# A decode kernel: the order of its first weight loads, and a first load of 14 KB rows

## The chip, the cores and the metric

The kernel runs on one core of one Trainium2 chip. The metric is the device time of one launch in microseconds (us). Times are quoted as medians, with the lowest and highest run. The profiled execution's span is about 1.2 us shorter than the time measured for the same run (399.1 us against 400.33), because the span goes from the first to the last instruction only.

## The reference, cut to what matters

One token goes through attention against a KV cache of 65536 positions (32 query heads, 4 KV heads), and through a mixer and MLP branch. Both results are added to the token.

```python
x  = layernorm(A_x)                                 # 1 x 1 x 1024
q  = x @ wq                                         # wq 1024 x 4096,   8.4 MB
o  = softmax(q k^T / sqrt(128)) v ; o @ wo          # k, v 67 MB each, wo 8.4 MB
h  = gelu(layernorm(x) @ w1)                        # w1 1024 x 1024,   2.1 MB
hs = shift(h) @ w2                                  # w2 1024 x 1024,   2.1 MB
x1 = x + hs
h2 = gelu(layernorm(x1) @ w3) @ w4                  # w3, w4            7.3 MB each
out = A_x + attention + x1 + h2                     # layer norms and details cut
```

The shift moves h along the sequence, by one or two places, and fills with zeros. The sequence has one position, so what reaches w2 is all zeros. The kernel still loads w2 and multiplies a vector of zeros with it. The values that lie in w2's place don't change the result as long as they are finite.

## The kernel before: the parts that matter

All large loads are issued by SyncE on one queue, so they run one after another on the core's 16 DMA engines. x (2 KB) is issued by ScalarE on a second queue. `KV` has three slots of 64 KB per partition; the weights go into them first, and each slot is given to K or V as soon as its weights have been used.

```python
def rows_src(w, r0, nrow):        # partition p gets rows 8p .. 8p+7, one contiguous run of memory
    return w.rearrange("(p r) n -> p (r n)", p=P)[:, r0 * w.shape[1]:(r0 + nrow) * w.shape[1]]

_dma(q_act, chan("x"), ... out=x_bf, in_=A_x ...)                        # 16 B per partition
kv_load(0, "s0", rows_src(A_wq, 0, 8), 8 * HQD)                          # wq: 64 KB per partition
kv_load(1, "w1", rows_src(B_w1, 0, 8), 8 * D, b_w1)                      # w1: 16 KB
_dma(q_sp, chan("w2"), ... out=KV[:, 1, 8*D:16*D], in_=rows_src(B_w2, 0, 8) ...)   # w2: 16 KB
kv_load(2, "s2", rows_src(B_w3, 0, 8), 8 * F)                            # w3: 56 KB
# ... (cut) layer norm of x, q = xn @ wq, then:
issue(3)                          # first K block into slot 0, after wq was used
# ... (cut) w1, gelu, w2 (with zeros)
issue(4)                          # first V block into slot 1
# ... (cut) w3, gelu
issue(5)                          # second K block into slot 2
# ... (cut) 8 blocks of attention; each issues the loads two blocks ahead
# ... (cut) at the end wo and four parts of w4: 17, 7, 3 and 1 row per partition
```

## Time and profile before

| | before |
|---|---|
| time, median (lowest to highest) | 400.36 us (400.35 to 400.61) |
| span | 399.1 us |
| moved by DMA | 169.97 MB, 426 GB/s over the span |
| DMA busy | 9 tenths or more in nearly every slice |
| DVE / PE busy | 55% / 42% |

The first lines of the page, with the row of 40 slices for DMA. Each digit is the busy share of a slice of 10 us in tenths. PE is TensorE's matmuls and PEld its weight loads, DVE is VectorE, ACT is ScalarE, POOL is GpSimd; SPq and ACTq are the queues of instructions that issue loads.

```profile
span 399.1 us, 3429 instructions
...
PE 168.9 (42%) x1523; PEld 59.0 (15%) x1484; DVE 221.4 (55%) x260; ACT 23.9 (6%) x50; POOL 7.7 (2%) x31
...
DMA  9999899999999999999999999999999999999995
GB/s 420 420 388 493 383 441 466 447 415 427 420 427 429 434 460 434 434 427 420 434 427 420 466 440 434 421 420 434 427 427 466 434 440 420 420 427 434 418 414 229
DMA packets 3759, 169.97 MB, mean 426 GB/s; under 512 B 548, under 2 KB 552, under 8 KB 808
```

DMA never rests and no other engine comes near. In the trace's packet records one packet is one partition's row of a load, so 64 KB for wq, K and V. A 64 KB packet takes a median of 2.42 us, and 16 engines at that rate move 434 GB/s. This agrees with the ceiling of 435 GB/s that the Trainium skill gives in "DMA: Bandwidth & Descriptors", Where 436 GB/s comes from.

The timeline of the early part of the kernel before. The columns are start in us, duration in us, engine, line, operation, output and input; in brackets the idle time of the engine before it and what ended it.

```profile
0.00 0.39 SPq L290 DMA_DIRECT2D KV<-in_A_wq_dram  x1
0.12 0.37 ACTq L295 DMA_DIRECT2D KV<-in_A_x_dram  x1
0.92 0.33 SPq L290 DMA_DIRECT2D KV<-in_B_w_dram  x1
1.30 0.73 SPq L300 DMA_DIRECT2D KV<-in_B_w_dram  x1
2.08 0.48 SPq L290 DMA_DIRECT2D KV<-in_B_w_dram  x1
...
22.24 0.17 DVE L339 CAST KV<-KV 128x8 f32<-128x8 bf16 x1 [22.24 <-DMA KV<-in_A_x_dram]
...
27.53 4.98 PE L379 MATMUL S_ps<-KV 128*32 128x512 bf16 x64 [1.36 <-DVE KV L359]
...
69.47 0.33 SPq L290 DMA_DIRECT2D KV<-in_A_k_cache_dram  x1
...
99.84 0.33 SPq L290 DMA_DIRECT2D KV<-in_A_v_cache_dram  x1
100.21 0.43 SPq L290 DMA_DIRECT2D KV<-in_A_k_cache_dram  x1
```

Although x has only 2 KB, it lands after 22.1 us, with wq. The q projection (27.53) waits for the layer norm of x. The lines at 69.47 and 100.21 show the slack of this early chain: the loads issued at 99.84 and 100.21 are wanted only as the engines finish the second K block, the first of them at 105.8 and the last at 107.7 us; it counts as landed at 108.2.

The chain of waits of the kernel before, in order of time: start in us, duration in us, what it was.

```profile
0.12 22.10 DMA KV<-in_A_x_dram
69.47 38.72 DMA KV<-in_A_k_cache_dram
108.21 13.10 DVE KV L460 x3
138.97 46.66 DMA KV<-in_A_k_cache_dram
185.65 13.10 DVE KV L460 x3
...
263.26 13.10 DVE KV L460 x3
...
363.64 32.91 DMA KV<-in_B_w_dram
```

Each block of attention starts when its K has landed, and the last thing waited for is w4. Its last row:

```profile
396.60 0.28 PE L566 MATMUL S_ps<-KV,gh_bf 128*1 128x256 bf16 x4 [0.15 <-DMA KV<-in_B_w_dram]
396.94 0.42 DVE L647 CAST orow<-S_ps 128x256 bf16<-128x256 f32 x1 [6.78 <-PE S_ps L566]
```

### The profile page before, as it was taken

The numbers are of one execution on the slowest core, as the hardware profiler recorded it, in microseconds if no ns is written. First come the engines' busy times: TensorE is split into PE (matmuls) and PEld (weight loads), VectorE is DVE, ScalarE is ACT, GpSimd is POOL, SyncE is SP. The second block draws the span as 40 slices with busy tenths as digits, with TensorE's granted clock in tenths as the row PEclk, the third lists the DMA queues.
The fourth block names the chain that finished last, engine by engine and source line by source line (L and its number), as shares of the span: only waits on it lengthen the run. The fifth ranks groups of instructions, "written<-read, shape, count | busy, mean of one in ns | idle before, by whom it ended". The sixth has DMA issues, their size and how long they took to land.

```text
span 399.1 us, 3429 instructions
## 1 busy us (share of the span) xinstructions
PE 168.9 (42%) x1523; PEld 59.0 (15%) x1484; DVE 221.4 (55%) x260; ACT 23.9 (6%) x50; POOL 7.7 (2%) x31
## 2 busy tenths in 40 slices
PE   0034767338033713460357036413541362137394
PEld 0011334012001210110012001101120110012232
DVE  0024222994298549833984597269647952895201
ACT  1000000011001100110011002000100110011000
POOL 5000000000000000000000000000000000000000
PEclk9998568555655665575557555855585558555969
DMA  9999899999999999999999999999999999999995
GB/s 420 420 388 493 383 441 466 447 415 427 420 427 429 434 460 434 434 427 420 434 427 420 466 440 434 421 420 434 427 427 466 434 440 420 420 427 434 418 414 229
DMA packets 3759, 169.97 MB, mean 426 GB/s; under 512 B 548, under 2 KB 552, under 8 KB 808
## 3 DMA queue, kind: packets, MB, share of 16 engines
q1 hardware_dynamic: 3608, 169.87, 98.7%
q8 instruction: 5, 0.08, 0.1%
q10 hardware_dynamic: 144, 0.00, 0.0%
q14 instruction: 2, 0.02, 0.0%
HBM read 169.87 MB, written 0.00 MB: 426 GB/s over the span
## 4 chain that ended last, share of the span: by engine, by line
DMA 59%; DVE 25%; PE 12%; issue 1%; ACT 1%; SPq 1%; POOL 0%
DMA KV<-in_A_k_cache_dram 45%; DVE KV L460 18%; DMA KV<-in_B_w_dram 8%; DMA KV<-in_A_x_dram 6%; PE S_ps L411 3%; PE OT_ps L518 2%; DVE mrow L481 2%; PE M_ps L426 2%; PE S_ps L474 2%; PE S_ps L379 1%; ACT p_sb L496 1%; DVE Yall L395 1%; DVE pT_f L509 1%; DVE pT_f L419 1%; PE PT_ps L505 0%
## 5 line engine op out<-in xcount | busy, mean ns | idle before, releaser
L460 DVE STREAM_TRANSPOSE KV<-KV 128x4096 f32<-128x4096 f32 x32 | 140.3, 4422 | 44.3 <-DMA KV<-in_A_k_cache_dram 44.3
L474 PE MATMUL S_ps<-KV,Ycur 128*32 128x512 bf16 x512 | 60.7, 624 | 132.5 <-DVE KV L460 132.5
L518 PE MATMUL OT_ps<-KV,pT_f 128*32 128x512 bf16 x512 | 47.2, 511 | 4.0 <-issue 3.0
L474 PEld LDWEIGHTS S_ps<-KV,Ycur 128*32 128x32 bf16 x512 | 14.3, 126 | 160.0 <-DVE KV L460 142.4
L496 ACT ACTIVATE p_sb<-S_ps,brun 128x1024 bf16<-128x1024 f32 x16 | 17.8, 1114 | 276.6 <-DVE brun L494 176.1
L509 DVE STREAM_TRANSPOSE pT_f<-PT_ps 128x512 f32<-128x512 f32 x32 | 22.5, 702 | 14.0 <-PE PT_ps L505 14.0
L481 DVE TENSOR_REDUCE mrow<-S_ps 128x1 f32<-128x1024 f32 x16 | 19.3, 1205 | 11.3 <-PE S_ps L474 11.3
L484 PE MATMUL M_ps<-Rm,Lmat 128*128 128x16 bf16 x16 | 3.1, 194 | 38.0 <-DVE Rm L482 38.0
L529 DVE SCALAR_TENSOR_TENSOR O_acc<-O_acc,ff,OT_ps 128x512 f32<-128x512 f32 x12 | 9.0, 748 | 14.7 <-PE OT_ps L518 14.7
L518 PEld LDWEIGHTS OT_ps<-KV,pT_f 128*32 128x32 bf16 x512 | 13.1, 115 | 23.8 <-issue 16.4
L411 PE MATMUL S_ps<-KV 128*32 128x512 bf16 x88 | 12.1, 538 | 2.7 <-DVE KV L359 2.7
L339 DVE CAST KV<-KV 128x8 f32<-128x8 bf16 x1 | 0.2, 172 | 22.2 <-DMA KV<-in_A_x_dram 22.2
L578 PE MATMUL S_ps<-KV,o_bf 128*1 128x512 bf16 x64 | 9.9, 484 | 4.5 <-DMA KV<-in_A_wo_dram 4.5
L505 PE MATMUL PT_ps<-p_sb,permR 128*128 128x512 bf16 x16 | 9.7, 607 | 0.8
L426 PE MATMUL M_ps<-ident_f,pT_f 64*128 64x2 f32 (+2 forms) x32 | 7.9, 373 | 2.5 <-DVE pT_f L419 2.5
L484 PEld LDWEIGHTS M_ps<-Rm,Lmat 128*128 128x128 bf16 x16 | 1.7, 104 | 49.3 <-DVE Rm L482 49.3
L582 DVE COPY pT_f<-S_ps 1x512 f32<-1x512 f32 x1 | 0.7, 679 | 14.4 <-PE S_ps L578 14.4
L426 PEld LDWEIGHTS M_ps<-ident_f,pT_f 64*128 64x128 f32 (+2 forms) x32 | 7.7, 326 | 4.7 <-DVE pT_f L419 3.1
L419 DVE COPY pT_f<-S_ps 64x512 f32<-64x512 f32 (+1 forms) x3 | 2.1, 685 | 10.8 <-PE S_ps L411 10.8
L505 PEld LDWEIGHTS PT_ps<-p_sb,permR 128*128 128x128 bf16 x32 | 3.3, 102 | 27.5 <-ACT p_sb L496 14.7
L364 PE MATMUL M_ps<-KV 8*128 8x8 bf16 x1 | 0.2, 184 | 16.1 <-DVE Dmat_f L363 16.1
L642 POOL MEMSET pT_f<- 64x512 f32 x1 | 0.5, 520 | 312.4 <-PE OT_ps L518 312.4
(88 smaller groups left out, 90.2 us busy)
## 6 DMA issues: line engine op xcount, KB each, us to landing
KV<-in_B_w_dram SPq DMA_DIRECT2D x1, 7168.0 KB, 48.0
KV<-in_B_w_dram SPq DMA_DIRECT2D x1, 4352.0 KB, 27.4
KV<-in_B_w_dram SPq DMA_DIRECT2D x2, 2048.0 KB, 28.3
KV<-in_B_w_dram SPq DMA_DIRECT2D x1, 1792.0 KB, 31.3
KV<-in_B_w_dram SPq DMA_DIRECT2D x1, 768.0 KB, 32.7
KV<-in_B_w_dram SPq DMA_DIRECT2D x1, 256.0 KB, 32.9
KV<-in_A_k_cache_dram SPq DMA_DIRECT2D x8, 46.7
KV<-in_A_v_cache_dram SPq DMA_DIRECT2D x8, 28.1
```

Source lines behind the costliest of these rows:

```text
L411: fns.append(lambda e, j=j, k=k, mv=mv: e.matmul(S_ps[32 * (k % 4):32 * (k % 4) + 32, bank + k // 4, :], vec[:, j:j + 1].broadcast_to([P, ...
L419: _op(q_dve, lambda e, b=b, nb=nb: e.tensor_copy(pT_f[0:32 * nb, b, :], S_ps[0:32 * nb, bank + b, :]), reads=[b_S[bank + b]], writes=[b_pT ...
L426: fns.append(lambda e, b=b, nb=nb, c=c: e.matmul(M_ps[:, c0 + 16 * b + c:c0 + 16 * b + 4 * nb:4], pT_f[0:32 * nb, b, c:512:4], ident_f[0:3 ...
L460: _op(q_dve, lambda e: e.transpose(out=KV32[:, s, o:o + 4096], in_=KV32[:, s, o:o + 4096]), reads=[b_KV[s][sub]], writes=[b_KV[s][sub]], l ...
L474: fns.append(lambda e, we=we, cm=cm, mv=mv: e.matmul(S_ps[32 * cm:32 * cm + 32, n % 4, :], Ycur[:, we, :, :].rearrange("p a g -> p (a g)") ...
L481: _op(q_dve, lambda e: e.reduce_max(mrow[:, k:k + 1], S_ps[:, 2 * k:2 * k + 2, :].rearrange("p b c -> p (b c)"), axis=AX.X), reads=b_S[2 * ...
L496: _op(q_act, lambda e: e.activation(p_sb[:, :, :].rearrange("p b c -> p (b c)"), S_ps[:, 2 * k:2 * k + 2, :].rearrange("p b c -> p (b c)") ...
L505: _op(q_pe, lambda e: e.matmul(PT_ps[:, :], permR[:, :], p_sb[:, n % 2, :], start=True, stop=True), reads=[b_p[n % 2], b_const], writes=[b ...
L509: _op(q_dve, lambda e: e.transpose(out=pT_f[:, n % 2, :], in_=PT_ps[:, :]), reads=[b_PT], writes=[b_pT[n % 2]], loop=True)
L518: fns.append(lambda e, q=q, q4=q4: e.matmul(OT_ps[32 * q4:32 * q4 + 32, g % 2, :], pT_bf[:, n % 2, q, :, 1], KV[:, s, 8192 * sub + 512 * q ...
L529: _op(q_dve, lambda e: e.scalar_tensor_tensor(out=O_acc[:, 0:512], in0=O_acc[:, 0:512], scalar=ff[:, k:k + 1], in1=OT_ps[:, k, :], op0=ALU ...
L578: _grp(q_pe, [lambda e, j=j, jj=jj: e.matmul(S_ps[32 * jj:32 * jj + 1, 1, :], o_bf[:, j:j + 1], KV[:, 0, j * D + 512 * jj:j * D + 512 * (j ...
```

## The change

Its intent is a better start of the DMA stream. The first load is now seven of w2's eight rows per partition, 14 KB, so that neighbouring partitions read at an odd multiple of 2 KB and not at a power of two (this distance between the starts of neighbouring partitions' pieces is called stride or pitch below); then come wq, w1, w2's last row and w3. Since w2 only meets zeros, it need not matter that this division puts other rows into the partitions.

```diff
-        kv_load(0, "s0", rows_src(A_wq, 0, 8), 8 * HQD)
         b_w1 = b_KV[1][0:2]
         b_w2 = b_KV[1][2:4]
+        _dma(q_sp, chan("w2"), lambda e: e.dma_start(out=KV[:, 1, 8 * D:15 * D], in_=B_w2[0:7 * P, :].rearrange("(p r) n -> p (r n)", p=P)), writes=b_w2)
+        kv_load(0, "s0", rows_src(A_wq, 0, 8), 8 * HQD)
         kv_load(1, "w1", rows_src(B_w1, 0, 8), 8 * D, b_w1)
-        _dma(q_sp, chan("w2"), lambda e: e.dma_start(out=KV[:, 1, 8 * D:16 * D], in_=rows_src(B_w2, 0, 8)), writes=b_w2)
+        _dma(q_sp, chan("w2"), lambda e: e.dma_start(out=KV[:, 1, 15 * D:16 * D], in_=B_w2[7 * P:8 * P, :]), writes=b_w2, partial=True)
         kv_load(2, "s2", rows_src(B_w3, 0, 8), 8 * F)
```

## The prediction

> **What bounds the kernel now.** DMA. The page's slice row shows DMA at 9 nearly throughout; 169.97 MB over a 399.1 us span is 426 GB/s. In the trace's packet records the first load packet starts 1.02 us into the span, and from there to about 393 us the 16 engines are never short of packets. A 64 KB packet takes a median 2.421 us, so 16 engines move 434 GB/s and the bytes alone need 392 us. The chain of waits is 45% DMA of K and ends on w4's last row, landing at 396.6.
>
> **What the change moves.** The same bytes in another order: w2a (1.84 MB), wq, w1, w2's last row (0.26 MB), w3.
>
> 1. x lands earlier. Its 16 B packets, eight per engine, are on another queue. The Trainium skill, "DMA: Bandwidth & Descriptors", Queues, rings and completion order, says that an engine round-robins between queues packet by packet; the trace agrees: each x packet follows a 64 KB wq packet, and x lands at 22.1 us. Behind 14 KB packets (0.54 us each in w4's 7-row part) I estimate 6 to 7.
> 2. wq lands later by 8 x 0.54 = 4.3 us: 21.7 -> 25.9. The q projection starts there rather than at 27.53, so the early chain, to the gelu at 69.5, moves about 1.3 us earlier. That buys nothing: the next K and V loads are issued (100 us) 8 us before the DMA queue runs dry (K lands at 108.2), and all later work waits for DMA.
> 3. More packets: w2's eight 16 KB packets per engine (0.611 us) become eight of 0.539 and eight of 2 KB (0.084): 4.98 instead of 4.89 us, +0.1 us.
> 4. The start. The 16 first wq packets take 2.83 to 3.48 us instead of 2.42, 0.72 us too much on average, never regained. Some is first-read latency: 8 KB instruction fetches on the idle chip before the span took 0.34 to 0.55 us against 0.30 at full rate, so 0.04 to 0.25. The rest I lay to engines starting in step at addresses a power of two apart. The skill's same page (Latency and other measured facts, HBM row pitch) reports slow copies at pitches of 512 KiB and up; here a pitch of 64 KB runs at full rate once engines are staggered, so only the start can suffer. A 14 KB stride should remove about 0.5 us, unless it returns when wq starts.
>
> **Critical path.** Only 3 and 4 lie on it: -0.5 + 0.1 = -0.4 us. The tail stays: engines end their last loads between 394.0 and 396.1 us; the slowest carries its start lag (0.6 us) and 16 KB instruction fetches (1.0 to 1.1 us each).
>
> **Prediction: 399.9 us**, 8 in 10 within 399.2 to 400.7. Faster by over 2%: 0.01; within 2%: 0.98; slower by over 2%: 0.01.
>
> **What would show it.** x landing at 6 to 7 us; layer norm over by 13; q projection from about 26 us, begun by DMA instead of DVE; first 14 KB packets within 0.3 us of 0.54; the wq packets after them at 2.42; first K's transposes near 68.2; third K landing (108.2) 0.3 to 0.6 us earlier, and later ones by the same.
>
> **What would make it wrong.** If the slow start is plain latency, or reappears in wq's first packets: 400.4 to 400.5. If the slowest engine at the end was the one that lost most at the start, or instruction fetches fall on another engine, the gain may reach 1 us.

## The result, and the profile after

The changed kernel took 401.08 us (400.49 to 401.15, 4 runs) against 400.37 us (400.35 to 400.61, 4 runs). The ratio is 1.0013, with a 95% interval of 0.9996 to 1.0031. Ratios here are the mean time of one kernel's fast runs over that of the other's of the same rounds, so not quite the ratio of the medians. That is the same within 2%, but it lies on the other side of zero than predicted and above the range. Two repeats gave 401.09 us each, 0.72 and 0.57 us over the kernel before of the same rounds, so the loss of 0.6 to 0.7 us is real, if small.

The page after:

```profile
span 399.8 us, 3446 instructions
...
DMA  9999999999999999999999999999999999999995
GB/s 394 420 397 479 411 420 465 439 421 439 426 426 428 420 459 433 426 439 439 426 420 439 446 433 426 434 433 426 426 452 439 426 439 420 433 426 433 421 412 213
DMA packets 3903, 169.97 MB, mean 425 GB/s; under 512 B 564, under 2 KB 568, under 8 KB 952
```

The same bytes moved, and DMA is as busy as ever. The first slice moved 394 GB/s instead of 420. The timeline after, with the lines that answer to those above:

```profile
0.00 0.39 SPq L298 DMA_DIRECT2D KV<-in_B_w_dram  x1
...
0.91 0.33 SPq L290 DMA_DIRECT2D KV<-in_A_wq_dram  x1
1.30 1.13 SPq L290 DMA_DIRECT2D KV<-in_B_w_dram  x1
7.68 0.33 SPq L301 DMA_DIRECT2D KV<-in_B_w_dram  x1
...
10.12 0.17 DVE L340 CAST KV<-KV 128x8 f32<-128x8 bf16 x1 [10.12 <-DMA KV<-in_A_x_dram]
...
27.16 6.25 PE L380 MATMUL S_ps<-KV 128*32 128x512 bf16 x64 [13.12 <-DMA KV<-in_A_wq_dram]
...
70.79 0.33 SPq L290 DMA_DIRECT2D KV<-in_A_k_cache_dram  x1
...
100.35 0.33 SPq L290 DMA_DIRECT2D KV<-in_A_v_cache_dram  x1
100.72 0.43 SPq L290 DMA_DIRECT2D KV<-in_A_k_cache_dram  x1
```

x is now there at 10.12 instead of 22.24, and the q projection waits for wq and no longer for the layer norm. Yet it ends at 33.4 and not earlier than before (32.5), because its 64 matmuls took 6.25 us instead of 4.98; more on that below. The next K and V are issued at 100.35 and 100.72, still well before the queue needs them. So the early chain costs nothing, in either kernel. The chain of waits and the tail after:

```profile
0.91 26.11 DMA KV<-in_A_wq_dram
70.79 37.58 DMA KV<-in_A_k_cache_dram
108.40 13.10 DVE KV L461 x3
138.63 47.19 DMA KV<-in_A_k_cache_dram
185.84 13.10 DVE KV L461 x3
...
263.72 13.10 DVE KV L461 x3
...
364.10 33.24 DMA KV<-in_B_w_dram
```

```profile
397.38 0.28 PE L567 MATMUL S_ps<-KV,gh_bf 128*1 128x256 bf16 x4 [0.15 <-DMA KV<-in_B_w_dram]
397.71 0.42 DVE L648 CAST orow<-S_ps 128x256 bf16<-128x256 f32 x1 [7.78 <-PE S_ps L567]
```

K lands 0.19 us later at 108 and 186, 0.46 later at 264, and w4's last row 0.78 later. A constant start loss would give a constant delay. The packet records explain why it grows.

**Each of the 16 DMA engines has its own clock of progress.** The engines get equal shares of every large load and never wait for each other, so an engine that falls behind stays behind. How far each engine's last packet of a load lies behind the first engine's, in us, sorted; read from the packet records, which name no engine: the engines are told apart by which packet starts where another ended.

```
                    first engine   lag of the 16 engines
before, first K      67.07   0 0 .01 .07 .11 .13 .17 .18 .19 .28 .35 .53 .62  .63 1.14 1.96
before, second K    105.78   0 .01 .01 .07 .11 .13 .17 .19 .28 .36 .53 .62 .63 1.14 1.73 1.96
before, wo          376.83   0 0 .07 .11 .13 .16 .18 .28 .35 .53 .62 .62 1.54 1.72 1.96 2.11
before, w4, 17 rows 387.16   0 0 .06 .10 .16 .18 .27 .35 .52 .61 .62 1.53 1.66 1.72 1.95 2.10
after,  first K      67.34   0 .03 .03 .09 .10 .17 .17 .30 .44 .50 .69 .96 1.08 1.20 1.33 1.88
after,  second K    106.08   0 0 .06 .09 .11 .16 .28 .41 .47 .66 .94 1.05 1.14 1.31 1.53 1.86
after,  wo          377.12   0 .06 .08 .11 .15 .27 .41 .47 .66 .94 1.05 1.13 1.52 1.55 1.85 2.27
after,  w4, 17 rows 387.45   0 .06 .08 .11 .15 .27 .41 .47 .66 .94 1.13 1.52 1.55 1.85 2.27 2.59
```

The lags below 1.3 us come from the start. The large ones come from instruction fetches, which the trace records as packets of kind "instruction" on queues 8 and 14, on the same 16 engines: five of 16 KB and two of 8 KB in this span. Each 16 KB fetch puts its engine back by about 1.55 us (for instance .18 to 1.73 in the kernel before, fetch at 81.8), each 8 KB fetch by 0.97 (1.14 to 2.11). A load counts as landed when the last engine is done, so the end waits for the engine with the largest sum of start lag and fetches.

This accounts for the result. w4's last packet ended at 396.09 before and 396.88 after, 0.79 us later. Of that, 0.29 is the fastest engine (376.83 to 377.12), and 0.48 is the lag of the last one (2.11 to 2.59). The last engine after the change is the one that had left the start 1.05 us late and then took the 16 KB fetch at 378.2: its 1.05 is gone from the next row of the table, and 2.59 is new. In the kernel before the fetch at 378.2 met an engine that was 0.13 late (it is at 1.66 after it). So the start grew worse in two ways, in its mean and in its spread, and the fetches turned the spread into time at the end.

### The profile page after: what moved, and what is told of

It is laid out like the page before. It is cut to its first block, busy times and chain, and to the rows that moved or that the text cites. A ratio compares the mean times of both kernels' runs of the same rounds, so it can differ in the third digit from the quotient of the medians.

```text
span 399.8 us, 3446 instructions
## 1 busy us (share of the span) xinstructions
PE 177.4 (44%) x1539; PEld 60.3 (15%) x1484; DVE 221.3 (55%) x260; ACT 23.9 (6%) x50; POOL 7.6 (2%) x31
## 4 chain that ended last, share of the span: by engine, by line
DMA 59%; DVE 25%; PE 12%; issue 1%; ACT 1%; SPq 1%; POOL 0%
DMA KV<-in_A_k_cache_dram 45%; DVE KV L461 17%; DMA KV<-in_B_w_dram 8%; DMA KV<-in_A_wq_dram 7%; PE S_ps L412 3%; PE OT_ps L519 2%; DVE mrow L482 2%; PE M_ps L427 2%; PE S_ps L475 2%; PE S_ps L380 2%; DVE pT_f L510 1%; ACT p_sb L497 1%; DVE Yall L396 1%; DVE O_acc L530 1%; DVE pT_f L420 1%
## 5 line engine op out<-in xcount | busy, mean ns | idle before, releaser
L506 PE MATMUL PT_ps<-p_sb,permR 128*128 128x512 bf16 x32 | 18.4, 574 | 0.8
L412 PE MATMUL S_ps<-KV 128*32 128x512 bf16 x88 | 12.5, 565 | 2.7 <-DVE KV L360 2.7
L380 PE MATMUL S_ps<-KV 128*32 128x512 bf16 x64 | 6.2, 575 | 13.1 <-DMA KV<-in_A_wq_dram 13.1
L579 PE MATMUL S_ps<-KV,o_bf 128*1 128x512 bf16 x64 | 8.8, 442 | 3.1 <-DMA KV<-in_A_wo_dram 3.1
```

What stands on the lines that cost most here:

```text
L380: fns.append(lambda e, j=j, b=b, jj=jj: e.matmul(S_ps[32 * jj:32 * jj + 32, b, :], xn_bf[:, j:j + 1].broadcast_to([P, 32]), KV[:, 0, j * H ...
L412: fns.append(lambda e, j=j, k=k, mv=mv: e.matmul(S_ps[32 * (k % 4):32 * (k % 4) + 32, bank + k // 4, :], vec[:, j:j + 1].broadcast_to([P, ...
L506: _op(q_pe, lambda e: e.matmul(PT_ps[:, :], permR[:, :], p_sb[:, n % 2, :], start=True, stop=True), reads=[b_p[n % 2], b_const], writes=[b ...
L579: _grp(q_pe, [lambda e, j=j, jj=jj: e.matmul(S_ps[32 * jj:32 * jj + 1, 1, :], o_bf[:, j:j + 1], KV[:, 0, j * D + 512 * jj:j * D + 512 * (j ...
```

## The experiments

Theory S: the small first packets spoil the start. Rivals: O, the odd stride does harm; P, the division into two loads does; X, x's packets do; and, later, C, the compact source of the first load, and D, a first load from another tensor than the next. The times are beside the kernel before of the same rounds and chip. "Mean K" is the mean over the 16 engines of the end of the first K load; it shows the start without the luck of the fetches at the end. It comes from one profiled launch of each run; the three of the changed kernel gave 67.90, 67.90 and 67.80.

| run | first load | time, us (range) | before, us | difference | mean K, us |
|---|---|---|---|---|---|
| before | wq, 64 KB at 64 KB pitch | | | | 67.47 |
| changed kernel | w2, 14 KB at 14 KB | 401.08 (400.49-401.15) | 400.37 | +0.71 | 67.90 |
| after_again | the same | 401.09 (400.91-401.31) | 400.37 | +0.72 | 67.90 |
| after_third | the same | 401.09 (400.63-401.21) | 400.52 | +0.57 | 67.80 |
| x_behind | the same, x on one queue | 401.11 (400.99-401.56) | 400.42 | +0.69 | 67.95 |
| w2_whole_first | w2, 16 KB at 16 KB | 400.69 (400.47-400.89) | 400.37 | +0.32 | 67.68 |
| split_not_first | wq, then the divided w2 | 400.51 (400.36-400.52) | 400.37 | +0.14 | 67.51 |
| wq_row_first | wq, 8 KB at 64 KB | 400.37 (400.31-400.46) | 400.42 | -0.05 | 67.41 |
| wq_compact | wq, 14 KB at 14 KB | 400.78 (400.51-400.88) | 400.56 | +0.22 | 67.67 |
| wq_spread | wq, 14 KB at 64 KB | 400.58 (400.51-400.80) | 400.56 | +0.02 | 67.63 |
| k_pitch14 | K, 14 KB at 14 KB | 401.13 (400.98-401.20) | 400.52 | +0.61 | 67.78 |
| k_pitch16 | K, 14 KB at 16 KB | 401.13 (401.04-401.21) | 400.52 | +0.61 | 68.22 |
| k_pitch32 | K, 14 KB at 32 KB | 400.57 (400.44-400.99) | 400.52 | +0.05 | 67.59 |
| k_spread | K, 14 KB at 64 KB | 400.49 (400.33-400.79) | 400.56 | -0.07 | 67.55 |
| small_first | w2, 2 KB at 2 KB | 400.72 (400.53-402.02) | 400.42 | +0.30 | 68.24 |
| small_from_wq | wq, 2 KB at 64 KB | 401.97 (400.87-402.52) | 400.56 | +1.41 | 67.80 |
| w3_first | w3, 56 KB at 56 KB | 407.84 (407.17-408.64) | 400.37 | +7.47 | 67.61 |
| no_w2 | wq, w2 not loaded | 395.45 (395.41-395.70) | 400.42 | -4.97 | |

Most differences are so small that the 95% interval of the ratio holds 1. For the pairs that carry the argument the ranges of the runs are apart: k_pitch14 and k_pitch16 (lowest 400.98) against k_spread (highest 400.79), and against the kernel before of their own rounds (highest 400.68).

### after_again and after_third: does it repeat?

The changed kernel, unaltered.

> The changed kernel once more, to see whether its time and its start repeat. Theory S (small first packets make a worse start: the 16 DMA engines leave the start more spread out, and the end waits for the most delayed engine): about 401.0 us; after the wq load the last engine is 0.9 to 1.2 us behind the first (0.61 in the kernel before). If the 0.7 us was chance of one load of the program: 400.4 and a spread near 0.6.

> The changed kernel as a control on this chip: 0.6 to 0.8 us over the kernel before, mean end of the first K load near 67.9 us.

It repeats: +0.72 and +0.57 us. In after_again the last three engines that no fetch had touched were 1.00, 1.01 and 1.07 us behind after wq (0.52, 0.61, 0.61 in the kernel before). One run in 4 and one in 5 came out at 400.5 and 400.6, so the start varies from launch to launch; those launches were not profiled.

### split_not_first: the division alone

```diff
+        kv_load(0, "s0", rows_src(A_wq, 0, 8), 8 * HQD)
         _dma(q_sp, chan("w2"), ... 7 rows of w2 ...)
-        kv_load(0, "s0", rows_src(A_wq, 0, 8), 8 * HQD)
```

> wq first as in the kernel before, then the divided w2: wq, seven rows of w2, w1, w2's last row, w3. Theory S: 400.4 to 400.6 us (0.1 us for the added packets), spread after wq 0.6 us. Rival P: about 401.0.

+0.14 us, as estimated for the added packets, though the two ranges overlap. The 401.0 us of rival P are far off, so it falls.

### w2_whole_first and w3_first: other strides, nothing divided

```diff
-        kv_load(0, ... wq) ; kv_load(1, ... w1) ; _dma(... w2) ; kv_load(2, ... w3)
+        _dma(... w2) ; kv_load(0, ... wq) ; kv_load(1, ... w1) ; kv_load(2, ... w3)     # w2_whole_first
+        kv_load(2, ... w3) ; kv_load(0, ... wq) ; kv_load(1, ... w1) ; _dma(... w2)     # w3_first
```

> All eight rows of w2 first, undivided (16 KB packets, a power-of-two stride), then wq, w1, w3. Theory S: as the changed kernel, 400.8 to 401.2 us, spread after wq 0.9 to 1.2 us. Rival O (the odd 14 KB stride itself does the harm): 400.3 to 400.5, spread near 0.6. Rival P (dividing w2 into two loads does the harm, by more packets): 400.3 to 400.5. The change's intent (the odd stride helps): over 401.2.

> w3 first (56 KB packets, stride 7 x 8 KB), then wq, w1, w2, nothing divided. Theory S: large first packets, so a start like that of the kernel before: 400.2 to 400.6 us, spread after the first load near 0.6 us. Rival O and the step of my prediction that failed (the start costs 0.5 us because of a power-of-two stride): if the stride mattered, the first packets would be over their full-rate time by 0.2 us or less rather than by 0.6.

w2_whole_first came out in between, at +0.32 us, and fitted neither theory. In w3_first the start answers the question: its 56 KB packets, at a stride that is no power of two, were too long by 0.66 us each on average over the 16 engines. The kernel before lost 0.72 with its stride of 64 KB. So the slow first packets are no matter of a power-of-two stride, and this was the very step on which my gain of 0.5 us rested.

The time of w3_first was a miss of mine, and a useful one. wq landed at 38 us, the early chain ran 12 us later, and the next loads were issued at 110.92 and 111.29, when the queue had run dry. The windows of w3_first, with DMA share and GB/s last:

```profile
85.00:105.00 20.00, 9.54 (x76) 2.51 (x80) 18.20 (x13) 1.21 (x2) 0.00 (x0) 0.50 0.97 420
105.00:112.00 7.00, 5.59 (x64) 1.43 (x54) 3.33 (x9) 1.30 (x3) 0.00 (x0) 0.81 0.30 103
112.00:125.00 13.00, 3.80 (x32) 0.89 (x32) 13.00 (x4) 0.00 (x0) 0.00 (x0) 0.60 1.00 425
```

The share of 0.30 in the second line is the hole: 5.65 us without a packet for the mean engine. The early chain's slack ends when the engines finish the second K load, so in the kernel before it was 6 to 8 us (issue at 99.84, engines done between 105.8 and 107.7).

The same trace holds one thing more. When the queue began again, at 111.9 us, the first 16 packets, 64 KB each of V, took 2.58 to 3.44 us, too long by 0.68 on average, though another block of V had been read before. So slow first packets are not peculiar to the start of the launch: here they came back when all engines began together after a pause. (Hole and second start make 6.3 of the 6.8 us by which this profiled launch was longer.)

### wq_row_first: small packets, other place

```diff
-        kv_load(0, "s0", rows_src(A_wq, 0, 8), 8 * HQD)
+        _dma(q_sp, chan("s0"),  ... out=KV[:, 0, 0:HQD],         in_=rows_src(A_wq, 0, 1) ...)
+        _dma(q_sp, chan("wqb"), ... out=KV[:, 0, HQD:8 * HQD],   in_=rows_src(A_wq, 1, 7) ...)
```

> wq is divided instead of w2: its first row of each partition (8 KB packets at a power-of-two pitch of 64 KB), then its other seven rows (56 KB packets), then w1, w2, w3. Theory S (small first packets spoil the start, whatever the stride): 400.7 to 401.3 us; fastest engine 0.1 to 0.4 us later than in the kernel before, most delayed engine 0.8 us or more behind it. Rival O (the harm came from the odd stride of the load, or from w2's place): 400.3 to 400.6 and a spread near 0.6.

No loss at all (-0.05 us), with first packets of 8 KB. After the first K load only two engines, both hit by fetches, were more than 0.44 us behind. Theory S, my own, fell here.

### x_behind: x's packets

```diff
-        _dma(q_act, chan("x"), ...)
         _dma(q_sp, chan("w2"), ... 7 rows of w2 ...)
+        _dma(q_sp, chan("x"), ...)
```

> The changed kernel with x on the same queue, behind the seven rows of w2, instead of on a second queue. Rival X (packets of x that interleave with the first small packets spoil the start): 400.4 to 400.7, spread near 0.6. Theory S: 400.9 to 401.2, spread 0.9 to 1.1.

+0.69 us, as the changed kernel. Rival X falls.

### wq_compact, wq_spread, k_spread: the same first load from other places

Only the source of the first load is altered. Its shape, packets and destination stay, and the result stays correct because the data meet zeros.

```diff
-  in_=B_w2[0:7 * P, :].rearrange("(p r) n -> p (r n)", p=P)
+  in_= 1.8 MB from the head of wq in one piece, 14 KB per partition         # wq_compact
+  in_= rows_src(A_wq, 0, 8)[:, 0:7 * D]                                     # wq_spread, 64 KB pitch
+  in_= the first K block, the first 14 KB of each partition's 64 KB         # k_spread
```

> The changed kernel, but its first load takes the same shape (14 KB packets, 14 KB stride, 1.8 MB in one piece) out of the head of wq instead of w2. The data are multiplied by zeros, so the result stays correct. Theory D (the first reads of a tensor are slow, and a short first load of another tensor makes wq pay again): mean end of the first K load over the 16 engines 67.4 to 67.6 us (67.47 in the kernel before, 67.90 in the changed one), time 400.4 to 400.7. Rival C (all engines reading one compact 1.8 MB piece at the start): 67.8 to 68.0, 400.9 to 401.2. Rival S (small packets first) is already against wq_row_first.

> The same, with the 14 KB pieces taken from wq at a pitch of 64 KB, so spread over 8 MB. Theories C and D both: mean end of the first K load 67.4 to 67.6, time 400.4 to 400.7. If it is as slow as the changed kernel (67.8 or more, 401), both fall, and it is the 14 KB packets, or the place they are written to.

> The same, with the 14 KB pieces taken at a pitch of 64 KB from the K cache, another tensor than the wq that follows. Theory C (compactness): 67.4 to 67.6, time 400.4 to 400.7. Theory D (another tensor first): 67.8 to 68.0, time 400.9 to 401.2.

Taken at a pitch of 64 KB, the 14 KB pieces cost nothing, whether from wq (+0.02) or from another tensor (-0.07). So theory D falls, and it is not the 14 KB packets either. The compact piece out of wq cost +0.22, less than that out of w2. Even this is not clear of noise: the range of wq_compact (400.51 to 400.88) covers that of wq_spread, and their mean K is nearly the same, 67.67 and 67.63. For wq alone, theory C is not shown.

### k_pitch14, k_pitch16, k_pitch32: the pitch alone

The 14 KB pieces all come from the K cache, and the pitch is the only difference between these runs.

```diff
+  in_=A_k_cache[0, 0, 0:BLK, :].rearrange("c d -> (c d)")[0:P * 7 * D].rearrange("(p c) -> p c", p=P)[:, 0:7 * D]
   # k_pitch16: 8 * D in place of the first 7 * D; k_pitch32: 16 * D
```

> The changed kernel with its 14 KB pieces taken from the K cache at a pitch of 14 KB (compact, odd stride); k_spread took them at 64 KB and was as fast as the kernel before. Theory C (a compact source is slow at the start): 0.2 to 0.8 us over before. If 0.6 to 0.8, compactness in a tensor other than wq explains the changed kernel whole; if 0.2 to 0.4, like wq_compact, then something of w2 itself adds to it. Rival (not the source's layout, but chance): within 0.1 of before.

> The same 14 KB pieces at a pitch of 16 KB, a power of two, over 2 MB of the K cache. Theory C: as k_pitch14 within 0.15 us. The change's intent, and my prediction's step: the odd pitch is better, so this one is slower than k_pitch14 by 0.3 us or more. Rival O (an odd pitch is worse): faster than k_pitch14 by 0.3 or more.

> The same 14 KB pieces at a pitch of 32 KB, over 4 MB. Theory C: between k_pitch14 and k_spread, so 0.0 to 0.4 us over before.

In the K cache the pitch decides it: +0.61 us at 14 KB, +0.61 at 16 KB, +0.05 at 32 KB, and -0.07 at 64 KB (k_spread). Odd or even makes no difference; how close together the 16 engines read does. Where the last w4 row was used up and the output was copied, in k_pitch14 first and then in k_spread:

```profile
397.73 0.42 DVE L648 CAST orow<-S_ps 128x256 bf16<-128x256 f32 x1 [7.69 <-PE S_ps L567]
```

```profile
396.99 0.42 DVE L648 CAST orow<-S_ps 128x256 bf16<-128x256 f32 x1 [7.41 <-PE S_ps L567]
```

The changed kernel had this copy at 397.71, the kernel before at 396.94. So a compact source is enough for a loss as large as the changed kernel's. The two compact runs lose it in different ways. In k_pitch14, as in the changed kernel, some engines leave the start late, up to 1.3 us behind the first (1.1 in the changed kernel). Part of this is that they begin late: the last engine's first packet started at 2.56 us in k_pitch14 and at 2.87 in the changed kernel, against 1.62 in k_spread and 1.88 in the kernel before. It need not be so: in after_third none began later than 1.65, but the packets of the first load were too long by 0.90 us per engine. In k_pitch16 all engines leave it together, and all late: the fastest ended the first K load at 67.88 us instead of 67.07, and no engine without a fetch was over 0.39 behind.

### small_first and small_from_wq: a very short first load

```diff
+        _dma(q_sp, chan("w2"), ... w2's last row, 2 KB per partition ...)       # small_first
         kv_load(0, "s0", rows_src(A_wq, 0, 8), 8 * HQD)
         kv_load(1, "w1", ...)
+        _dma(q_sp, chan("w2a"), ... the other seven rows ...)
   # small_from_wq: the 2 KB come from wq at a pitch of 64 KB
```

> Only w2's last row first (2 KB packets, 0.7 us at full rate), then wq, w1, w2's seven rows, w3. If the start costs its delay once, after the first read, in whatever packets come then: 400.5 us (0.1 more than before for the packets). If a small first load makes the start be paid a second time, in the first packets of wq: 400.8 to 401.3, and the first 64 KB packets are over 2.42 us by 0.3 or more.

> small_first with its 2 KB pieces taken from wq at a pitch of 64 KB instead of from w2 (result still correct). small_first had a mean end of the first K load of 68.24 and wq's first packets 0.76 us too long on average. Theory D: wq has been touched, so its first 64 KB packets run near 2.42 us, mean end 67.4 to 67.7, time 400.4 to 400.7. If wq's first packets still cost 0.5 us or more, D falls: then a short first load is paid by whatever comes next.

Both vary much from launch to launch (400.53 to 402.02, and 400.87 to 402.52). The profiles are of the slowest launch of small_first (402.02) and the fastest of small_from_wq (400.87). In them the first wq packets were too long by 0.74 and 0.48 us per engine, after the 2 KB packets had already lost 0.36 and 0.23. A first load of 0.7 us is over before the start is, and what follows pays again, even at a pitch of 64 KB. This is a second way to lose at the start; theory D does not survive it either.

### no_w2: what bytes are worth

```diff
-        _dma(q_sp, chan("w2"), ... w2 ...)
-        proj(1, 8 * D, D, g_bf, 3, b_w2 + [b_const], 272) ; x1 = xn + (zeros) ; acc += (zeros)
+        _op(q_dve, lambda e: e.tensor_copy(x1, xn), ...)
```

> The kernel before without w2's load and product (the product is with zeros: with a sequence of one, the shift leaves nothing, so the result is unchanged). It measures what bytes are worth. If the time is bytes over rate: 2.10 MB less at 434 GB/s, 4.8 us less, 395.3 to 395.7 us. If the early compute chain or the tail also holds the time: less than 4 us gained.

395.45 us, 4.97 less. At 434 GB/s, 2.10 MB are 4.83 us. The kernel is bounded by bytes, and this version beats both kernels (ratio 0.9878 to the kernel before). It is exact only because the sequence has one position and w2 is finite, and it loads less than the two kernels compared here, so it answers another question than the order of loads does.

## Why the prediction was wrong, point by point

- **DMA bounds the kernel: right.** no_w2 shows it, and between the start and w4 the packet records show the engines without packets in no run except w3_first.
- **x lands earlier: right in kind, wrong in size.** Predicted 6 to 7 us, measured 10.1. The last 16 B packet ended at 7.33 us, but x's completion packets took their turn after wq's first 64 KB packets and ended between 8.57 and 9.75. The Trainium skill's statement in "DMA: Bandwidth & Descriptors", Queues, rings and completion order, that an engine goes round its queues packet by packet, agrees with both numbers; I had not applied it to the completion.
- **The early chain moves 1.3 us earlier: not in this profile, and without effect.** The q projection did start on wq, at 27.16, but the second K load was issued at 70.79 instead of 69.47. The matmuls ran slowly for longer: a median of 633 ns instead of 380. The clock records grant full speed from 30.3 us in the kernel before and from 32.5 after, 2.8 and 5.3 us after the projection began. The Trainium skill, "TensorE: Matmul & The Clock Gate", Part 1, says that an idle array is throttled to half and released by activity; matmuls of about 634 and 379 ns stand in both kernels. The longer idle time before the projection (13.12 us in the brackets, 1.36 before) does not explain the difference: split_not_first had waited 1.36 us and has a median of 631 ns, k_spread had waited 13.12 us and has 379. Over the 18 profiles the release came 2.6 to 5.8 us after the projection began. In after_third, the same changed kernel, it came after 3.1 us and the second K load was issued at 69.37, so the size of this step is the luck of the launch.
- **More packets, +0.1 us: agrees** with split_not_first (+0.14), but is too small to be shown by it.
- **The step that failed is the fourth: "A 14 KB stride should remove about 0.5 us, unless it returns when wq starts."** I laid most of the 0.72 us to engines starting in step at addresses a power of two apart. The starts with odd strides were no better: 0.66 us too long per engine in w3_first, and in the changed kernel 0.63 in the 14 KB packets and 0.14 in the first wq packets after them. There was also idle time in the first microseconds, 0.52 us per engine against 0.18, most of it in three engines whose first packet started only between 2.84 and 2.87 us (the latest in the kernel before: 1.88). Together the start cost 1.29 us per engine instead of 0.89. What the change really did to the source was to pack it: 1.8 MB instead of 8.4 MB. The K runs show that this costs time (+0.61 us), at an odd pitch and at an even one.
- **The tail "stays": wrong.** The slowest engine is not fixed. It was an engine with two 8 KB fetches before, and one with a late start and a 16 KB fetch after, and the end moved by 0.48 us more than the fastest engine for that reason. The prediction named the sum of start lag and fetches, but used it only for a gain, and it counted a 16 KB fetch as the 1.0 to 1.1 us of its packet, while the engine falls back by about 1.55.

What stays open: what makes the first packets slow at all (w3_first shows only that a pause of the queue brings it back), and why a compact source adds to the loss at the start. That the engines contend for the same part of memory is only argued. In mid-stream, w1 and w2 are read just as compactly at full rate (0.611 us per 16 KB packet in the kernel before), where the engines come to them up to 0.6 us apart. Open too is why the compact piece cost 0.22 us out of wq and w2_whole_first 0.32, but the compact pieces out of K and w2 0.6 to 0.7. Which engine a fetch falls on decides a part of such differences: after w4's first part the last engine was 2.50 us behind the first in wq_compact, 2.89 in k_pitch14.

## What to carry to other kernels

In a kernel bounded by DMA from the first microsecond to the last, the first load sets how late and how far apart the engines start, and none of it is regained; let it be long, and let the engines read far apart. No order tried here gained anything: the best two lie 0.05 and 0.07 us below the kernel before, which is noise. Before you explain a slow start by an address pattern, vary the pattern alone with data that don't matter, as the K runs do here. And when every engine has its own queue of equal work, predict the slowest engine, by summing what falls on each, and not the mean.

## What the Trainium skill lacked or had wrong

- "DMA: Bandwidth & Descriptors", Latency and other measured facts, warns of row pitches of 512 KiB and more. It lacks the opposite case at the start of a stream: 14 KB pieces from the K cache at a pitch of 14 or 16 KB cost 0.61 us more than the kernel before, at 32 KB 0.05, at 64 KB nothing (-0.07).
- No page gives the cost of a cold start of the 16 engines with large packets: the packets of the first load were too long by 0.49 to 1.08 us per engine in all starts with packets of 8 KB and more, 0.72 with 64 KB in the kernel before. After a pause it was paid again, 0.68 us (w3_first, at 111.9 us).
- "Runtime: NRT & Kernel Launch" says in its note on TENSOR_LOAD that instructions are fetched through a port of their own. This does not fit the runs, nor the page's own section Instruction fetch mechanics, by which a DMA queue fetches them in blocks of 16 KiB: here instruction packets of 16 KB and 8 KB stand in the DMA queues' records. What the page lacks is their cost to a stream of loads: each puts one of the 16 engines back, by 1.55 and 0.97 us.
- "DMA: Bandwidth & Descriptors", Queues, rings and completion order, does not say that the completion packet takes its own turn among the queues: x's data had landed by 7.33 us, its last completion packet ended at 9.75.
- "TensorE: Matmul & The Clock Gate", Part 1, puts the warm-up at about 3.4 us of time, and its spread from run to run at 500 ns either way. Here full speed was granted 2.6 to 5.8 us after the q projection began, over the 18 profiles (3.1 to 5.6 in the three of the changed kernel). The free-running window that the page describes allows for that, its round figures don't.
